# Gated mix of two attentions on one core: the output as f32r products of halves, two octets of a block at a unit's end

## The chip, the cores and the metric

The kernel runs on one core of one Trainium2 chip. The metric is the device time of one execution in microseconds (us). The engines are named as the profile names them: PE (TensorE; its weight loads apart as PEld), DVE (VectorE), ACT (ScalarE), POOL (GpSimd) and SP (SyncE), on which nearly all DMAs are issued. SP issues its DMAs in the order of the program.

## The reference

```python
x = A_x                                            # 1 x 2048 x 512, f32
g = sigmoid((x * gate_w).sum(-1, keepdims=True))
a = attention(x, A_wqkv) @ A_wo                    # 32 heads of 16, full softmax over 2048 keys
b = memory_attention(x, B_wq, B_wk, B_wv) @ B_wo   # 32 heads of 16, four segments of 512 tokens
return g * a + (1 - g) * b
...
# memory_attention, in segment s: causal softmax inside the segment, and a memory of the segments before
o = sig(beta) * (phi(q) @ M) / (phi(q) @ z + 1e-6) + (1 - sig(beta)) * (p @ v)
M = M + phi(k).T @ v; z = z + phi(k).sum()
```

Everything is computed in float32 precision. Where the kernel uses PE's f32r type, an operand is split into a half that f32r holds and a half with the rest, and a product is three matmuls: low by high, high by low, high by high.

## The kernel before

**Stages.** A first stage (to about 320 us) projects x to q, k and v of both sides as three f32r products of halves and writes them to DRAM. The main stage then runs *units*: a unit is one side (A or B), a group g of four heads (0 to 7) and a segment c of 512 query tokens (0 to 3). The units alternate A, B, A, B through the groups of a segment, then the next segment. An A unit has 64 *slots*, a B unit 10; `nS` is the count of all slots. In slot n PE computes one score tile (L645, `st`), of which ACT takes the exponential (L668, `p`), and the score product for a maximum of slot n + 96 (L197, into one of the four `sm` banks), which DVE reduces (L212 for side A, L222 for side B). So every unit's maxima are made 96 slots before its scores. When all maxima of a unit stand, POOL splits them in two halves (L179, L180, `ms`), PE transposes them (L188), ACT copies (L191, `mt`), and SP writes them as further rows into the unit's q (L194, "the rows"); the unit's scores need these rows.

**Bursts.** Every third slot ends a *burst*: there PE computes either values (p times v, L701, up to three or four entries of 128 keys, summed in the bank `ops`) or, if output work is waiting in the list `shared`, four pieces of that; beside it up to one entry of the list `fill` whose slot has come. In the last segment `jam` raises the number of value entries more readily. In `wide`, 60 slots after the last maximum (from slot nS - 94 to nS - 34), a burst is six slots, with up to eight values and three entries of `fill`. Behind the last slot every step is a burst.

**Octets.** When the values of a unit are complete, ACT copies them from `ops`, and SP writes them (L706, `od`). After an odd group the *octet* o = g // 2 (eight heads, 128 rows of attention output) is finished by `octet` in four steps at given slots: SP reads the sums (L744, `rec`) and the values (L751); POOL computes the reciprocal and the factors (L760 to L766) and SP writes them (L767, `rd`); SP reads them spread over the rows (L771, `inv`); POOL multiplies (L774), and on side B adds the memory's part (L776), which after an even B group comes by the same steps as octet "M". The results stay in SBUF, in the tiles `held`.

**Output.** The output of 128 tokens, a *block*, sums over both sides and four octets. `piece` (L784) computes 128 x 128 of it for one octet of one side as four f32 matmuls of 32 tokens side by side in PE's columns; in the profile each such matmul shows as two records. At the end of each A unit of segments 1 to 3 half the columns (two of four pieces wide) of one block of the segment before are computed in `ops`: 16 pieces in four bursts; `leave` (L809) copies them with ACT and SP writes them. In the last segment the ends of six B units also carry output: two quarters of block 3 of segment 2, and octet 0 of the four blocks of the last segment, which `keep` (L817) copies to SBUF.

**Closing.** The rest of the last segment's output, octets 1 to 3, is summed in the four banks of the maxima, which are free by then: 96 pieces from the list `closing`, spread by `close` over `fill` from slot nS - 94 on. The last octet (A, 3) is finished by DVE instead of POOL at the very end; 16 pieces, four additions of the kept part and four writes follow it.

**Queues.** All of this is one program order per engine, written out by the loop at L860; `at(n, f)` (L730) puts f in front of slot n. Loads for a maximum are issued 20 slots ahead of it. Tiles of a tag rotate over its number of buffers, so that a new one waits until the old one's readers are done.

Of the kernel before, what the change touches and what calls it, by code (L numbers as in the profile page):

```python
# [10 lines left out]
F32 = mybir.dt.float32  # L11
# [8 lines left out]
D = 512  # L20
# [26 lines left out]
def gated_mix(ctx, tc, x, xT, wqkv, a_wo, b_wq, b_wk, b_wv, b_wo, beta, gate_w, out):  # L47
# [674 lines left out]
    minus = fr.tile([128, 32], F32, name="minus")  # L722
    nc.gpsimd.memset(minus, -1.0)
    held = {}
    scaled = set()


# [5 lines left out]
    def octet(side, o, c, t0, vector=False):  # L733

        hs = slice(8 * o, 8 * o + 8)
        sums, rows, eng = (dend[c][hs], rdM[c][hs], nc.gpsimd) if side == "M" else (od[side, c][hs, 16], rd[side, c][hs], nc.gpsimd)
        if vector:
            eng = nc.vector
        k = {}

        def load():
            assert side == "M" or {(side, 2 * o, c), (side, 2 * o + 1, c)} <= stored
            k["rec"] = fr.tile([128, 32], F32, tag="rec", name="rec", bufs=3)
            nc.sync.dma_start(k["rec"], sums.rearrange("h (q t) -> h q t", q=16))  # L744
            if side == "M":
                k["v"] = held["M", c, o] = fr.tile([128, CH], F32, tag="vM", name="vM", bufs=2)
            else:
                if (side, c) not in held:
                    held[side, c] = fr.tile([128, NO, CH], F32, tag="v" + side, name="v" + side, bufs=2)
                k["v"] = held[side, c][:, o]  # L750
            nc.sync.dma_start(k["v"], numd[c][:, o] if side == "M" else od[side, c][hs, 0:16].rearrange("h r t -> r h t"))  # L751

        def factors():
            rec = k["rec"]
            if vector:
                eng.reciprocal(rec, rec)
            else:

                r, e = (fr.tile([128, 32], F32, tag=t, name=t, bufs=2) for t in ("rcp", "err"))
                eng.tensor_tensor(r, rec, minus, op=ALU.pow)  # L760
# [6 lines left out]
            nc.sync.dma_start(rows.rearrange("h (q t) -> (h q) t", q=16), k["rec"])  # L767

        def factor():
            k["inv"] = fr.tile([128, CH], F32, tag="inv", name="inv", bufs=3)  # L770
            nc.sync.dma_start(k["inv"], heads(rows))  # L771

        def scale():
            eng.tensor_mul(k["v"], k["v"], k["inv"])  # L774
            if side == "B" and c:
                eng.tensor_add(k["v"], k["v"], held.pop(("M", c, o)))  # L776
            scaled.add((side, o, c))
        for n, f in ((0, load), (10, factors), (17, factor), (28, scale)):
            if t0 is None:
                f()  # L780
            else:
                at(t0 + n, f)

    def piece(ps, side, o, c, b, j, start, stop):  # L784

        assert (side, o, c) in scaled
        for t in range(4):
            nc.tensor.matmul(ps[32 * t:32 * t + 32, 128 * (j % (ps.shape[1] // 128)):128 * (j % (ps.shape[1] // 128)) + 128],  # L788
                             held[side, c][:, o, 128 * b + 32 * t:128 * b + 32 * t + 32], wos[side][:, o, 128 * j:128 * j + 128],
                             start=start, stop=stop, tile_position=(0, 32 * t))  # L790

    def out_rows(c, b):
        return out[c * CH + b * 128:c * CH + (b + 1) * 128, :]
# [1 line left out]
    fill = []  # L795
    shared = []

    def output(c, b, octets, cols, then, bank=ops):

        ps = bank[:, 0:128 * len(cols)]  # L800
        ks = [(side, o, j) for o in octets for side in "AB" for j in cols]
        for i, (side, o, j) in enumerate(ks):
            def f(i=i, side=side, o=o, j=j):
                piece(ps, side, o, c, b, j, i == 0, i == len(ks) - 1)
                if i == len(ks) - 1:
                    then(ps, c, b, cols)
            yield f

    def leave(ps, c, b, cols):  # L809
        w, j0 = 128 * len(cols), 128 * cols[0]  # L810
        t = fr.tile([128, D], F32, tag="res", name="res", bufs=2)
        nc.scalar.copy(t[:, 0:w], ps)
        nc.sync.dma_start(out_rows(c, b)[:, j0:j0 + w], t[:, 0:w])

    part = {}

    def keep(ps, c, b, cols):  # L817
        part[b] = fr.tile([128, D], F32, tag=f"part{b}", name="part")
        nc.scalar.copy(part[b], ps)

    last = NCH - 1
    between = {("A", g, c): (c - 1, g // 2, range(NO), range(2 * (g % 2), 2 * (g % 2) + 2), leave)
               for c in range(1, NCH) for g in range(NG)}
    del between["A", NG - 1, last]
    fill.extend((wide.start, f) for f in output(*between.pop(("A", NG - 2, last)), banks[0]))
    for j in (2, 3):
        between["B", j - 2, last] = (last - 1, 3, range(NO), (j,), leave)
    for b in range(4):  # L830
        between["B", b + 2, last] = (last, b, (0,), range(4), keep)

    for u in units[1:]:
        at(max(0, first[u] - 30), lambda u=u: load_v(u))
    at(100, lambda: load_wo("A", a_wo))
    at(180, lambda: load_wo("B", b_wo))


    closing = [(side, o) for o in range(1, NO) for side in "BA"]
    assert nS - 30 > nS - LEAD + 4  # L840
    def close(n, side, o, b, j):
        def f():
            piece(banks[b], side, o, last, b, j, (side, o) == closing[0] and j == 0, (side, o) == closing[-1] and j == 3)
        fill.append((n, f))
    early = [(k, 0) for k in closing[:4]]
    for (side, o), b in early + [(k, b) for k in closing[:-1] for b in range(4) if (k, b) not in early]:
        for j in range(4):
            close(max(wide.start if ((side, o), b) in early else nS - 30, end[side, 2 * o + 1, last] + 56), side, o, b, j)
# [11 lines left out]
    while n < nS or queue or beside or filled[0] < len(fill):  # L860
        for f in beside.pop(n, []):
            f()
        if n < nS:
            score_part(n)
        m = n + LEAD
        if m < nS:
            loads(m + PRE)

            max_part(m, lambda: banks[m % 4])
        run_todo(m)  # L870
        if n >= nS or n % (2 * BURST if n in wide else BURST) == (2 * BURST if n in wide else BURST) - 1:
            if shared:
                for _ in range(8 if n in wide else 4):
                    shared and shared.pop(0)()
# [18 lines left out]
    assert len(stored) == len(units)  # L893
    for b in range(4):
        for j in range(4):
            close(0, "A", NO - 1, b, j)
            fill.pop()[1]()
        t = fr.tile([128, D], F32, tag="vM" if b % 2 else "res", name="res", bufs=2)
        nc.vector.tensor_add(t, banks[b], part[b])
        (nc.scalar if b % 2 else nc.sync).dma_start(out_rows(last, b), t)  # L900


# [33 lines left out]
```

## Time and profile before

| | us |
|---|---|
| Time, median of 3 runs (lowest to highest) | 1841.38 (1839.18 to 1842.61) |
| Time of the profiled execution | 1840.35 |
| Span of its profile | 1838.6 |
| Mean granted clock of PE | 0.999 |

The busy time of PE, DVE, ACT and POOL in stretches of the main stage, of that execution:

| stretch, us | what runs | PE | DVE | ACT | POOL |
|---|---|---|---|---|---|
| 680 to 1440 (760.0) | segments 1 and 2 | 759.91 | 754.70 | 659.40 | 252.00 |
| 1440 to 1760.5 (320.5) | the last segment, while maxima are made | 320.50 | 312.82 | 272.18 | 111.78 |
| 1760.5 to 1796 (35.5) | no maxima any more; mostly `wide` | 33.30 | 0.00 | 32.92 | 17.50 |
| 1796 to 1817.5 (21.5) | the last scores and values | 21.40 | 0.00 | 17.27 | 4.89 |
| 1817.5 to 1838.6 (21.1) | the rest of the closing and the last octet | 17.16 | 4.00 | 0.59 | 0.00 |

How to read the lines of the profile: "L645" is line 645 of the kernel; "out<-in" are the tiles written and read; "x16" is a count; then come busy time, the mean duration of one in ns, and the idle time of the engine in front of it with what ended it. A line of a timeline begins with the start and the duration in us. SPq rows are the issues of DMAs. Ends of matmuls are modelled, those of DVE, ACT and POOL are not.

### The profile page before, as it was taken

What the parts mean: (1) busy time and instruction counts of PE and PEld (TensorE: products, weight loads), DVE (VectorE), ACT (ScalarE), POOL (GpSimd) and SP (SyncE); (2) the same over time, 40 slices, a digit from 0 to 9 for tenths busy, and PEclk for the clock granted to TensorE, in tenths of its full rate; (3) what the DMA queues carried; (4) which work ended last, traced back from release to release, by engine and by line L of the source; (5) the groups of instructions that cost most, each with busy time, mean ns of one, the idle gap of its engine ahead of it and who ended that gap; (6) DMA issues with size and microseconds to landing.
All of it is one profiled execution on the core that took longest, in us unless ns stands there. A gap on an engine that the chain in (4) does not pass through costs nothing.

```text
span 1838.6 us, 47838 instructions
## 1 busy us (share of the span) xinstructions
PE 1825.7 (99%) x18673; PEld 1001.6 (54%) x18673; DVE 1594.0 (87%) x3331; ACT 1447.4 (79%) x2772; POOL 518.1 (28%) x619
## 2 busy tenths in 40 slices
PE   9999999999999999999999999999999999999999
PEld 7888666545545545454444454444444455555545
DVE  4234677999999999999999999999999999999920
ACT  5445444788888888888888888888888888888894
POOL 3001222104040404242424242424232423242331
PEclk9999999999999999999999999999999999999999
DMA  7568645435343434344444343444344433342421
GB/s 234 195 224 263 210 175 171 137 112 136 89 109 93 113 86 116 103 108 111 111 103 117 103 116 104 116 104 116 104 105 115 116 106 91 107 114 85 114 66 49
DMA packets 124177, 227.40 MB, mean 124 GB/s; under 512 B 34952, under 2 KB 49960, under 8 KB 123440
## 3 DMA queue, kind: packets, MB, share of 16 engines
q1 hardware_dynamic: 122448, 222.68, 42.2%
q8 instruction: 148, 2.42, 0.6%
q0 software_dynamic: 1216, 1.14, 0.2%
q14 instruction: 77, 0.63, 0.1%
q10 hardware_dynamic: 288, 0.52, 0.1%
HBM read 155.52 MB, written 67.52 MB: 121 GB/s over the span
## 4 chain that ended last, share of the span: by engine, by line
PE 96%; ACT 2%; DVE 1%; POOL 1%; issue 0%; DMA 0%; SPq 0%; POOLq 0%; DVEq 0%; ACTq 0%
PE ops L701 32%; PE st L645 28%; PE sm L197 14%; PE pr L295 13%; PE ops L788 6%; PE sm L788 1%; POOL mn L355 1%; PE num L477 1%; ACT p L668 1%; PE mt_ps L188 0%; DMA raw<-wqkv 0%; PE mps L508 0%; ACT ex L362 0%; DVE jk L442 0%; ACT full L350 0%
## 5 line engine op out<-in xcount | busy, mean ns | idle before, releaser
L668 ACT ACTIVATE p<-st 128x512 f32<-128x512 f32 x2276 | 1198.2, 601 | 192.2 <-PE sm L197 149.1
L212 DVE TENSOR_REDUCE pm<-sm 128x1 f32<-128x512 f32 x2048 | 1266.6, 682 | 16.9 <-PE sm L197 16.4
L197 PE MATMUL sm<-kA,qA 48*128 48x512 f32 x2048 | 731.0, 445 | 0.0
L645 PE MATMUL st<-qA,kA 50*128 50x512 f32 x2029 | 668.0, 432 | 1.4 <-ACT mt L191 1.1
L701 PE MATMUL ops<-p,vA 128*17 128x384 f32 (+3 forms) x6872 | 555.3, 424 | 0.0
L645 PEld LDWEIGHTS st<-qA,kA 50*128 50x128 f32 x2029 | 330.7, 185 | 385.3 <-ACT p L668 320.8
L197 PEld LDWEIGHTS sm<-kA,qA 48*128 48x128 f32 x2048 | 332.9, 184 | 21.9 <-issue 7.1
L760 POOL TENSOR_TENSOR rcp<-rec,minus 128x32 f32<-128x32 f32 x43 | 234.1, 5445 | 181.9 <-DMA rec<-dend 137.5
L222 DVE CUSTOM_DVE_ANT_0 rest<-sm,mask 128x128 f32<-128x128 f32 (+3 forms) x512 | 247.9, 484 | 7.6 <-PE sm L197 0.8
L701 PEld LDWEIGHTS ops<-p,vA 128*17 128x17 f32 x6872 | 139.8, 96 | 194.8 <-issue 164.3
L649 POOL TENSOR_SCALAR_AFFINE_SELECT p<-p 128x512 f32<-128x512 f32 x128 | 79.5, 639 | 436.9 <-ACT p L668 433.0
L197 PE MATMUL sm<-kB,qB 48*128 48x128 f32 (+3 forms) x512 | 148.2, 349 | 0.0
L358 DVE TENSOR_TENSOR q<-full,q 128x512 fp32r<-128x512 f32 x64 | 44.4, 694 | 89.9 <-ACT q L351 89.9
L645 PE MATMUL st<-qB,kB 50*128 50x512 f32 (+1 forms) x495 | 109.8, 334 | 0.9 <-ACT p L668 0.9
L645 PEld LDWEIGHTS st<-qB,kB 50*128 50x128 f32 x495 | 70.1, 185 | 58.4 <-ACT p L668 51.4
L197 PEld LDWEIGHTS sm<-kB,qB 48*128 48x128 f32 x512 | 87.5, 186 | 6.4 <-DVE pm L212 2.7
L701 PE MATMUL ops<-p,vB 128*17 128x128 f32 (+3 forms) x1080 | 86.7, 425 | 0.1
L350 ACT COPY full<-pr 128x512 f32<-128x512 f32 x64 | 37.4, 584 | 53.2 <-PE pr L295 52.9
L355 POOL TENSOR_SCALAR mn<-full 128x512 f32<-128x512 f32 x24 | 36.3, 1512 | 101.7 <-ACT full L350 81.3
L788 PE MATMUL ops<-woA,vA 128*32 128x128 f32 x1600 | 64.3, 278 | 0.0
L179 POOL CAST ms<-pm 128x16 fp32r<-128x16 f32 x32 | 6.3, 198 | 204.5 <-DVE pm L222 204.5
L788 PE MATMUL ops<-woB,vB 128*32 128x128 f32 x1600 | 62.1, 273 | 0.0
(157 smaller groups left out, 1489.7 us busy)
## 6 DMA issues: line engine op xcount, KB each, us to landing
kA<-kdA SPq DMA_DIRECT2D x256, 128.0 KB
vA<-vdA SPq DMA_DIRECT2D x31, 544.0 KB
kA<-kdA SPq DMA_DIRECT2D x256, 64.0 KB
qdA<-q SPq DMA_DIRECT2D x32, 256.0 KB
kdA<-q SPq DMA_DIRECT2D x32, 256.0 KB
qdB<-q SPq DMA_DIRECT2D x32, 256.0 KB
qA<-qdA SPq DMA_DIRECT2D x64, 128.0 KB
kdB<-q SPq DMA_DIRECT2D x32, 256.0 KB
```

The costliest lines, as they stand in the source:

```text
L197: nc.tensor.matmul(ps[:, n0:n0 + n], rows(qt[u][:, :, s * 128:(s + 1) * 128], h, 48), rows(k[:, :, k0:k0 + n], h, 48), start=True, stop=True)
L212: nc.vector.tensor_reduce(pm[:, h, s, kc:kc + 1], ps, axis=AX.X, op=ALU.max)
L222: nc.vector.tensor_tensor_reduce(out=tri["rest"][:, 0:w], in0=ps[:, n0:n0 + w], in1=tri["mask"][:, CH - w:], scale=-1.0, scalar=3.0e38, op ...
L295: nc.tensor.matmul(ps, l(a, k), r(b, k), start=(n == 0), stop=(n == 11))
L355: nc.gpsimd.tensor_scalar_min(ph["mn"], full, 0.0)
L358: nc.vector.tensor_sub(q2, full, q1.bitcast(F32))
L645: nc.tensor.matmul(ps[:, n0:n0 + CH - q0], rows(k[:, :, b * 128:(b + 1) * 128], h, 50), rows(q[:, :, q0:], h, 50), start=True, stop=True)
L649: nc.gpsimd.affine_select(out=x, in_=x, pattern=[[0, 4], [1, 128]], base=0, channel_multiplier=-1, compare_op=ALU.is_ge, fill=0.0)
L668: nc.scalar.activation(p[:, h], ps, AF.Exp, scale=SCALE)
L701: nc.tensor.matmul(ops[32 * h:32 * h + 17, q0:q0 + 128 * w], v[:, 17 * h:17 * h + 17], p[:, h, c0:c0 + 128 * w], start=(i == 0), stop=done ...
L760: eng.tensor_tensor(r, rec, minus, op=ALU.pow)
L788: nc.tensor.matmul(ps[32 * t:32 * t + 32, 128 * (j % (ps.shape[1] // 128)):128 * (j % (ps.shape[1] // 128)) + 128], held[side, c][:, o, 12 ...
```

## The change

- `piece` goes. `products` computes the output over all 512 columns at once: for one octet of one side, three f32r matmuls of 128 x 128 weights (the octet's halves) and 512 columns (the halves of the output weights). A block takes 24 of them.
- `octet` ends with a cast and a subtraction that split its result into halves (tile `hl`), and SP writes them to DRAM (`hd`). `held` no longer keeps results in SBUF. The last octet's halves of both sides stay in SBUF.
- At the end of an A unit two octets of a block, not half the columns, are summed: 12 products in three bursts. SP loads their halves 20 slots before the unit's last slot (`load_block`). After an even group `keep` copies the sum to SBUF; after an odd one `leave` copies it, POOL adds the kept sum, and SP writes 128 x 512.
- The last segment's B units carry no output, and `jam` has no case of its own for it. Octet 0 of the last segment joins the closing (120 products with block 3 of segment 2 after the last maximum); the halves of octets 0 to 2 come back from DRAM to buffers of k and q (`load_closed`). `fill` gives four entries a burst in `wide` and behind the last slot, otherwise two.
- The output weights are loaded in eight parts and split by POOL during the first segment.
- At the very end two ACT copies and two DVE copies stand in place of the four additions.

```diff
+    hd = {(s, c): dr.tile([NO, 128, 4, 2, 128], F32, name=f"hd{s}{c}") for s in "AB" for c in range(NCH)}
...
-    def load_wo(side, w):
-        wos[side] = wo.tile([128, NO, D], F32, name=f"wo{side}")
-        nc.sync.dma_start(wos[side], w.rearrange("(o p) d -> p o d", p=128))
+    def load_wo(side, w, o, n):
+        k = {}
+        def load():
+            if o == 0:
+                wos[side] = wo.tile([128, NO, 2, D], F32R, name=f"wo{side}")
+            k["t"] = fr.tile([128, D], F32, tag="v", name="woraw", bufs=2)
+            nc.sync.dma_start(k["t"], w[128 * o:128 * o + 128])
+        def split():
+            h = wos[side][:, o]
+            nc.gpsimd.tensor_copy(h[:, 0], k["t"])
+            nc.gpsimd.tensor_sub(h[:, 1], k["t"], h[:, 0].bitcast(F32))
+        at(n, load)
+        at(n + 8, split)
...
         def scale():
             eng.tensor_mul(k["v"], k["v"], k["inv"])
             if side == "B" and c:
                 eng.tensor_add(k["v"], k["v"], held.pop(("M", c, o)))
+            if side == "M":
+                return
+            t = fr.tile([128, 4, 2, 128], F32R, tag="hl", name="hl", bufs=2)
+            for bs in (slice(0, 2), slice(2, 4)) if vector else (slice(0, 4),):
+                v = k["v"].rearrange("p (b t) -> p b t", b=4)[:, bs]
+                eng.tensor_copy(t[:, bs, 0], v)
+                eng.tensor_sub(t[:, bs, 1], v, t[:, bs, 0].bitcast(F32))
+            if o == NO - 1 and c == NCH - 1:
+                closed[side, o] = t
+            else:
+                nc.sync.dma_start(hd[side, c][o], raw(t))
             scaled.add((side, o, c))
...
-    def piece(ps, side, o, c, b, j, start, stop):
...
+    def products(ps, t, b, side, o, start, stop):
+        for i, (x, w) in enumerate(((1, 0), (0, 1), (0, 0))):
+            yield lambda i=i, x=x, w=w: nc.tensor.matmul(ps, t[:, b, x], wos[side][:, o, w], start=start and i == 0,
+                                                         stop=stop and i == 2)
...
+    def load_block(c, b, os):
+        assert all((side, o, c) in scaled for side in "AB" for o in os)
+        t = fr.tile([128, 2, 2, 2, 128], F32R, tag="blk", name="blk", bufs=2)
+        for i, side in enumerate("AB"):
+            nc.sync.dma_start(raw(t)[:, i, 0:len(os)].rearrange("p o h t -> p o (h t)"),
+                              hd[side, c][os[0]:os[-1] + 1, :, b].rearrange("o p h t -> p o (h t)"))
...
+    def keep(ps, c, b):
+        part[b] = fr.tile([128, D], F32, tag="part", name="part")
+        nc.scalar.copy(part[b], ps)
+
+    def leave(ps, c, b):
         t = fr.tile([128, D], F32, tag="res", name="res", bufs=2)
+        nc.scalar.copy(t, ps)
+        if b in part:
+            nc.gpsimd.tensor_add(t, t, part.pop(b))
+        nc.sync.dma_start(out_rows(c, b), t)
...
+    pairs = range(0, 2), range(2, 4)
+    between = {("A", g, c): (c - 1, g // 2, pairs[g % 2:g % 2 + 1], (keep, leave)[g % 2]) for c in range(1, NCH) for g in range(NG)}
+    for g in (6, 7):
+        del between["A", g, last]
+        at(wide.start - 24, lambda g=g: load_block(last - 1, 3, pairs[g % 2]))
+    fill.extend((wide.start, f) for f in output(last - 1, 3, pairs, leave, banks[0]))
+    for u, (c, b, (os,), _) in between.items():
+        at(end[u] - 20, lambda a=(c, b, os): load_block(*a))
...
+    closing = [(side, o) for o in range(NO) for side in "BA"]
+    def load_closed(side, o):
+        assert (side, o, last) in scaled
+        if o:
+            t = kbuf["A"][knext["A"] % NKA]
+            knext["A"] += 1
+        else:
+            t = qp.tile([128, 2, CH], F32R, tag="q", name="qclosed")
+        t = closed[side, o] = t.rearrange("p a (b h t) -> p (a b) h t", b=2, h=2)
+        nc.sync.dma_start(raw(t), hd[side, last][o])
+    for i, (side, o) in enumerate(closing[:6]):
+        at(nS - 82 + 2 * i, lambda side=side, o=o: load_closed(side, o))
...
-        if n >= first["A", 0, last]:
-            return (len(queue) > 6) + (len(queue) > 13)
...
-                for _ in range(3 if n in wide else 1):
+                for _ in range(4 if n in wide or n >= nS else 2):
...
-        t = fr.tile([128, D], F32, tag="vM" if b % 2 else "res", name="res", bufs=2)
-        nc.vector.tensor_add(t, banks[b], part[b])
+        t = fr.tile([128, D], F32, tag="v" if b % 2 else "res", name="res", bufs=2)
+        (nc.vector.tensor_copy if b % 2 else nc.scalar.copy)(t, banks[b])
         (nc.scalar if b % 2 else nc.sync).dma_start(out_rows(last, b), t)
```

More of the change, by code (lines that the diff above doesn't have):

```diff
@@ L724, in gated_mix @@
     held = {}
+    closed = {}
     scaled = set()
@@ L745, in load @@
             if side == "M":
-                k["v"] = held["M", c, o] = fr.tile([128, CH], F32, tag="vM", name="vM", bufs=2)
+                k["v"] = held["M", c, o] = fr.tile([128, CH], F32, tag="vM", name="vM")
             else:
-                if (side, c) not in held:
-                    held[side, c] = fr.tile([128, NO, CH], F32, tag="v" + side, name="v" + side, bufs=2)
-                k["v"] = held[side, c][:, o]
+                k["v"] = fr.tile([128, CH], F32, tag="v", name="v", bufs=2)
             nc.sync.dma_start(k["v"], numd[c][:, o] if side == "M" else od[side, c][hs, 0:16].rearrange("h r t -> r h t"))
@@ L769, in factor @@
         def factor():
-            k["inv"] = fr.tile([128, CH], F32, tag="inv", name="inv", bufs=3)
+            k["inv"] = fr.tile([128, CH], F32, tag="inv", name="inv", bufs=2)
             nc.sync.dma_start(k["inv"], heads(rows))
@@ L796, in gated_mix @@
     shared = []
[L798 to L810, printed above, removed]
-        t = fr.tile([128, D], F32, tag="res", name="res", bufs=2)
-        nc.scalar.copy(t[:, 0:w], ps)
-        nc.sync.dma_start(out_rows(c, b)[:, j0:j0 + w], t[:, 0:w])
@@ L815, in gated_mix @@
[L815 to L819, printed above, removed]
-    last = NCH - 1
[L824 to L829, printed above, removed]
@@ L830, in gated_mix @@
-    for b in range(4):
-        between["B", b + 2, last] = (last, b, (0,), range(4), keep)
+    blocks = []
+    def load_block(c, b, os):
[4 more added lines that the diff above has]
+                              hd[side, c][os[0]:os[-1] + 1, :, b].rearrange("o p h t -> p o (h t)"))
+        blocks.append(t)
+        loaded_blocks[c, b, os] = len(blocks)
@@ new lines, in gated_mix, with output, f @@
+    loaded_blocks = {}
+    def output(c, b, pairs, then, ps=ops):
+        ks = [(os, o, i) for os in pairs for o in os for i in range(2)]
+        for k in ks:
+            def f(n, k=k):
+                os, o, i = k
+                assert loaded_blocks[c, b, os] > len(blocks) - 2
+                t = blocks[loaded_blocks[c, b, os] - 1][:, i, o % 2].unsqueeze(1)
+                list(products(ps, t, 0, "AB"[i], o, k == ks[0], k == ks[-1]))[n]()
+                if k == ks[-1] and n == 2:
+                    then(ps, c, b)
+            for n in range(3):
+                yield lambda n=n, f=f: f(n)
@@ L839, in gated_mix @@
[L839 to L845, printed above, removed]
+    for i, (side, w) in enumerate((("A", a_wo), ("B", b_wo))):
+        for o in range(NO):
+            load_wo(side, w, o, 30 + 12 * (4 * i + o))
+    closing = [(side, o) for o in range(NO) for side in "BA"]
@@ L846, in gated_mix, with close, f @@
+    def close(n, side, o, b):
+        for i in range(3):
+            def f(i=i):
+                assert (side, o, last) in scaled
+                list(products(banks[b], closed[side, o], b, side, o, (side, o) == closing[0], (side, o) == closing[-1]))[i]()
+            fill.append((n, f))
+    early = [(k, 0) for k in closing[:6]]
     for (side, o), b in early + [(k, b) for k in closing[:-1] for b in range(4) if (k, b) not in early]:
-        for j in range(4):
-            close(max(wide.start if ((side, o), b) in early else nS - 30, end[side, 2 * o + 1, last] + 56), side, o, b, j)
+        close(nS - 66 if ((side, o), b) in early else max(nS - 30, end[side, 2 * o + 1, last] + 60), side, o, b)
@@ L872, in gated_mix @@
             if shared:
-                for _ in range(8 if n in wide else 4):
-                    shared and shared.pop(0)()
+                for _ in range(4):
+                    shared.pop(0)()
             else:
```

15 lines of the change are left out of this document (5 added, 10 removed).

## The prediction, made before the changed kernel ran

> **What bounds the kernel now.** I read the page first, then the busy time by stretches, then the timelines of PE, VectorE (DVE), GpSimd (POOL) and the SP queue around one end of a unit.
>
> ```profile
> PE 1825.7 (99%) x18673; PEld 1001.6 (54%) x18673; DVE 1594.0 (87%) x3331; ACT 1447.4 (79%) x2772; POOL 518.1 (28%) x619
> L212 DVE TENSOR_REDUCE pm<-sm 128x1 f32<-128x512 f32 x2048 | 1266.6, 682 | 16.9 <-PE sm L197 16.4
> ```
>
> PE's 99% says little, since the ends of matmuls are modelled. By stretches (length, then busy time of PE, weight loads, DVE, ACT, POOL) it is plainer:
>
> ```profile
> 680.00:1440.00 760.00, 759.91 (x8577) 372.79 (x8575) 754.70 (x1595) 659.40 (x1279) 252.00 (x291) 1.00 0.41 107
> 1440.00:1760.50 320.50, 320.50 (x4014) 163.34 (x4013) 312.82 (x667) 272.18 (x531) 111.78 (x127) 1.00 0.39 106
> 1760.50:1796.00 35.50, 33.30 (x428) 16.34 (x423) 0.00 (x0) 32.92 (x68) 17.50 (x17) 1.00 0.18 53
> 1796.00:1817.50 21.50, 21.40 (x241) 9.48 (x240) 0.00 (x0) 17.27 (x34) 4.89 (x7) 1.00 0.07 14
> 1817.50:1838.60 21.10, 17.16 (x606) 16.53 (x595) 4.00 (x7) 0.59 (x1) 0.00 (x0) 0.97 0.28 92
> ```
>
> From 680 to 1440 DVE idles 5.3 of 760 us, 0.7%: its maxima set the pace, and work taken from PE there is worth nothing. From 1440, the last segment, it idles 7.7 of 320.5 us, so there PE is part of the bound. After the last maximum (1760.5) PE and ACT share the bound, then PE alone, and the last 21 us are a chain of DMAs.
>
> **The change, part by part.** The profiled execution took 1840.35 us (span 1838.6); the median is 1841.38, and I add that 1.0 at the end.
>
> *One product against one piece.* A product is an f32r matmul of 128 rows, 128 columns of weights and 512 columns; the projections run the same shape, one behind the other (the 18 rows from the first shown to the last are one kind):
>
> ```profile
> 20.03 0.39 PE L295 MATMUL pr<-xh,wkl 128*128 128x512 f32 x1
> ...
> 23.89 0.39 PE L295 MATMUL pr<-xh,wkh 128*128 128x512 f32 x1
> ```
>
> ```profile
> L788 PE MATMUL ops<-woA,vA 128*32 128x128 f32 x1600 | 64.3, 278 | 0.0
> 1830.02 0.69 DVE L774 TENSOR_TENSOR vA<-vA,inv 128x512 f32<-128x512 f32 x1 [6.25 <-DMA inv<-rdA]
> 1830.77 3.92 PE L788 MATMUL sm<-woA,vA 128*32 128x128 f32 x128
> 1834.92 0.69 DVE L899 TENSOR_TENSOR res<-sm,part 128x512 f32<-128x512 f32 x1 [0.29 <-PE sm L788]
> ```
>
> Seventeen intervals in 3.86 us: 0.227 us a product. The last 16 pieces (128 records, eight a piece) took 3.92 us, less 0.28 for the last one's run-out: 0.228 a piece. So the two cost the same, and a block of 128 rows falls from 32 pieces to 24 products, 7.3 to 5.4 us.
>
> *Segments 1 and 2.* A unit's end gives one of four bursts back (four pieces, 0.91 us). DVE sets the pace there: 0. The wider evictions (512 columns for 256) lie on ACT, 659 of 760 us busy: 0.
>
> *Last segment.* B units' ends give no output any more, and A units' three bursts instead of four; the runs are then those of the other segments. If DVE comes to idle 0.7% here as well, 2.2 us, the segment gains 7.7 - 2.2 = **5.4 us**. It cannot gain more, and is worth 0 if something else holds PE.
>
> *After the last maximum.* Octet 0's products now also fall here. By the order of both programs, until the last values stand 24 pieces in eight bursts of the wide stretch and 12 behind, and in the new one 32 and 26. That is 8 x 0.227 = 1.8 us in the wide stretch, where PE is busy 33.3 and ACT 32.9 of 35.5 us, and 26 x 0.227 - 12 x 0.228 = 3.2 us behind it. One burst of each:
>
> ```profile
> 1789.14 1.91 PE L701 MATMUL ops<-p,vA 128*17 128x512 f32 x16
> 1792.53 1.91 PE L701 MATMUL ops<-p,vA 128*17 128x512 f32 x16
> 1800.35 0.40 PE L788 MATMUL sm<-woB,vB 128*32 128x128 f32 x8
> 1802.28 0.40 PE L788 MATMUL sm<-woB,vB 128*32 128x128 f32 x8
> ```
>
> A wide burst takes 3.39 us for six exponentials, a late one 1.93 for three; ACT is busy 17.3 of 21.5 us in the late ones and hides nothing. Bounds 3.2 and 5.0 us; I take **4.1**, half of the wide part hidden behind ACT.
>
> *The end.* After the last values the new program has 50 products in hand, 11.4 us, less than the 12.5 us from 1817.5 until the last factors are multiplied in (1830.02); the chain of DMAs stays the bound. Then come a cast and a subtraction of half a tile on DVE before the first product; by the 0.69 of a whole tile and some start-up, 0.8 us for the two; the second half lies behind products. Twelve products take 2.7 us against 3.9 of the pieces: 0.8 - 1.2 = **-0.4 us** (0 to -0.7).
>
> *The octets' halves, and whom they hold up.* This decides. At the end of an odd A unit POOL, SP and PE work like this (run of the unit ended at 1157.8; SP, then POOL, PE, DVE):
>
> ```profile
> 1157.82 0.34 SPq L706 DMA_DIRECT2D odA<-oraw  x1
> 1165.42 0.36 SPq L813 DMA_DIRECT2D out<-res  x1
> 1168.93 0.34 SPq L767 DMA_DIRECT2D rdA<-rec  x1
> 1171.80 1.02 SPq L771 DMA_DIRECT2D inv<-rdA  x1
> 1183.92 0.34 SPq L767 DMA_DIRECT2D rdB<-rec  x1
> 1187.55 0.53 SPq L771 DMA_DIRECT2D inv<-rdB  x1
> 1193.14 1.43 SPq L194 DMA_DIRECT2D qB<-mt  x2
> ```
>
> ```profile
> 1162.16 5.44 POOL L760 TENSOR_TENSOR rcp<-rec,minus 128x32 f32<-128x32 f32 x1
> 1175.43 1.28 POOL L774 TENSOR_TENSOR vA<-vA,inv 128x512 f32<-128x512 f32 x1 [6.53 <-DMA inv<-rdA]
> 1176.67 5.43 POOL L760 TENSOR_TENSOR rcp<-rec,minus 128x32 f32<-128x32 f32 x1
> 1190.98 1.29 POOL L774 TENSOR_TENSOR vB<-vB,inv 128x512 f32<-128x512 f32 x1 [2.29 <-DMA inv<-rdB]
> 1192.35 1.28 POOL L776 TENSOR_TENSOR vB<-vB,vM 128x512 f32<-128x512 f32 x1
> ```
>
> ```profile
> 1200.07 0.73 PE L197 MATMUL sm<-kA,qA 48*128 48x512 f32 x2
> 1200.41 0.64 PE L645 MATMUL st<-qB,kB 50*128 50x512 f32 x2
> ```
>
> ```profile
> 1201.24 3.08 DVE L212 TENSOR_REDUCE pm<-sm 128x1 f32<-128x512 f32 x5
> ```
>
> The maxima's rows (mt) are issued at 1193.14 and first read by PE's scores at 1200.41. The new program puts on SP, ahead of them, the write of the B octet's halves, which waits until POOL has multiplied, added, cast and subtracted. SP issues in order, so the rows wait too, and behind them the next keys; for the rows PE's scores wait, and behind these, in order, the maxima that feed DVE. How late? POOL's new operations: a 128x512 addition or subtraction 1.28; the cast has no row of its size. Bounds:
>
> ```profile
> L649 POOL TENSOR_SCALAR_AFFINE_SELECT p<-p 128x512 f32<-128x512 f32 x128 | 79.5, 639 | 436.9 <-ACT p L668 433.0
> L355 POOL TENSOR_SCALAR mn<-full 128x512 f32<-128x512 f32 x24 | 36.3, 1512 | 101.7 <-ACT full L350 81.3
> 818.29 0.34 SPq L767 DMA_DIRECT2D rdB<-rec  x1
> 819.73 0.53 SPq L771 DMA_DIRECT2D inv<-rdB  x1
> ```
>
> 0.64 to 1.51 us; I take 1.0, between the two operations of one input. The page GPSIMD Engine Reference of the Trainium skill (Engine selection) calls one-input operations roughly line-rate; L649's row bears that out, L355's, dearer than a two-input 1.28, does not; by the rule the cast would be near 0.64 and the sum below smaller by 0.7 a run.
>
> From a written row of factors to its reading back stand 1.44 us (818.29 to 819.73) to 3.63 (1183.92 to 1187.55); I take 2.0. Now the chain. The output leaves three slots sooner (3 x 0.616 by DVE's row, 1.85) with 0.2 more copying: 1165.42 - 1.85 + 0.2 = 1163.8. POOL adds the kept part, 1.28, ahead of A's reciprocal: 1165.1 instead of 1162.16. To the write of A's factors 6.77: 1171.9; reading begins 1173.9; the product 3.63 later, 1177.5; product, cast, subtraction 3.6: 1181.1. B's reciprocal to its factors 7.25: 1188.3; read 1190.3; product at 3.43 more, 1193.8; product, sum, cast, subtraction 5.05 with gaps: 1198.8. The write 0.4, then the rows' two issues from 1199.2; the second begins near 1199.9 and lands 1.44 later at the soonest: 1201.4 to 1202. PE wanted it at 1200.41: 1.0 to 1.6 us late. DVE is not empty at once: it has the 1200.07 products, until about 1201.85, and needs 0.6 after PE goes on, so the loss is the lateness less 0.9: 0.1 to 0.7 us. With both bounds taken low the lateness is -0.5 and the loss 0; with both high it is 5.6 and the loss 4.7. The late side reaches further: I take 0.8. The order of the new program has this write ahead of the rows in ten runs (four in segment 1, four in 2, two in 3): **+8 us**, 0 to 47. If the cover goes entirely, each further us of lateness costs 10.
>
> *Hidden edits.* The weights' 16 splits on POOL come in the first segment, 12 slots apart, where POOL is idle most of the time; block loads are issued 20 slots ahead with the DMA engines busy 0.41; A's write waits on a POOL result that is 3.6 us old when SP has issued the 16 loads in front: 0, as long as these covers hold.
>
> Sum: 1840.35 - 5.4 + 4.1 - 0.4 + 8 = 1846.7, and with the 1.0 to the median **1848 us**.
>
> **Rivals.**
> (a) *The write is in time.* Cast and readings back at their short ends: no loss. 1841.4 - 5.4 + 4.1 - 0.4 = 1839.7: no change. For it: the loss starts only 0.9 us behind the need. Against it: two bounds must both be short.
> (b) *Faster: PE's relief in the last segment.* As (a), and ACT covers the whole wide part, and the late bursts in part: from 1440 DVE idles 0.7%, 5.4 us, and the tail costs 1.2 or less. It decides from a tail cost below 2: 1837 down to 1835. For it: PE and ACT are within 0.4 us of each other in the wide stretch. Against: the late 3.2 us have no cover.
> (c) *A slow landing.* The rows land behind the 512 KB write in the same queue. In this trace a 16 KB read behind loads came late:
>
> ```profile
> 805.94 0.61 SPq L744 DMA_DIRECT2D rec<-odB  x1
> 811.04 5.43 POOL L760 TENSOR_TENSOR rcp<-rec,minus 128x32 f32<-128x32 f32 x1 [4.44 <-DMA rec<-odB]
> ```
>
> 5.1 us from issue to use. Behind the write I price it 1.2 us above the forecast's, so 10 x 2.0 = 20: 1860. The page DMA: Bandwidth & Descriptors of the Trainium skill (Queues, rings and completion order) has each engine's ring consumed in order, which is this rival; the row above fits it. Against: the rows are 16 KB in all, and the write may be half drained.
> That the products don't run as f32r can't be seen from before; both operands are written as f32r, and I give it nothing of its own.
>
> **Chances.** The forecast 0.38, (c) 0.14, (a) 0.28, (b) 0.20. About 0.2%, 3.7 us, is what a measurement of this kernel tells from no change; the forecast and (c) lie beyond it: slower 0.52, same 0.28, faster 0.20. Range: from (b)'s 1835 to somewhat above (c), where the unknown landing and cast reach, 1867; the forecast's own is 1844 to 1856.
>
> **What would show it.** Right: POOL's cast of 128x512 near 1.0; the rows' issue moved from 7.3 us ahead of the first B scores to about 1; in ten places PE's weight load of B scores waits for a DMA, and DVE idles some 8 us more from 680 on; DVE 99% busy in the last segment outside these places; late bursts of 2.2 us in place of 1.93; 1831.4 as the counterpart of the first product after 1830.02. Wrong: no wait of these scores for a DMA, or idle time of DVE behind POOL's maxima (ms) or block loads instead.

## The result, and the profile after

| | median us | runs | profiled execution: time, span |
|---|---|---|---|
| before | 1841.56 | 4 (1839.18 to 1842.61) | 1840.35, 1838.6 |
| changed | 1862.09 | 4 (1856.16 to 1869.18) | 1869.18, 1867.4 |

The ratio is 1.0115 (95% interval 1.0067 to 1.0163): slower by some 20 us, where 7 were forecast. The changed kernel's four runs lie 13 us apart, the two slower ones at the lower granted clock of PE: 1856.16 and 1856.48 at 0.994 and 0.995, 1867.70 at 0.989, 1869.18 at 0.986. The profile below is that of the last one, 7 us above the median.

The busy time by stretches, cut at the last maximum (columns: window, length, then PE, weight loads, DVE, ACT, POOL, then granted clock, DMA share, GB/s):

```profile
680.00:1440.00 760.00, 750.52 (x6986) 358.59 (x6984) 734.98 (x1552) 645.25 (x1246) 286.89 (x325) 0.98 0.46 126
1440.00:1777.90 337.90, 333.93 (x3150) 159.53 (x3148) 329.74 (x714) 289.57 (x560) 131.08 (x147) 0.99 0.47 129
1777.90:1867.40 89.50, 79.00 (x518) 37.89 (x518) 3.98 (x10) 52.46 (x104) 29.02 (x32) 0.94 0.29 97
```

From 680 to 1440 DVE issues 1552 instructions for 1595: its maxima, which set the pace before, now wait. The last maximum ends at 1777.9 for 1760.5, 17.4 us later, and the stretch behind it takes 89.5 us for 78.1, 11.4 more. Together that is the 28.8 us between the spans.

Who waits (engine, line, what it waited for: us in all, times, longest):

```profile
PE st L661 <- DMA qB<-mt: 11.9, 7, 2.5
PE mt_ps L191 <- POOL ms L183: 6.5, 2, 5.3
DVE pm L215 <- PE sm L200: 36.0, 31, 2.4
```

The first line is the forecast's wait: B scores for the maxima's rows. It was not in the profile of before at all. The second was only named as a sign of being wrong: PE's transposition of the maxima waits for POOL. DVE's waits for PE rose from 16.4 us by 19.6.

The odd run that the forecast walked through, now begun at 1163.86. SP:

```profile
1163.86 0.34 SPq L722 DMA_DIRECT2D odA<-oraw  x1
1178.14 0.34 SPq L782 DMA_DIRECT2D rdA<-rec  x1
1180.67 0.55 SPq L786 DMA_DIRECT2D inv<-rdA  x1
1194.68 0.34 SPq L782 DMA_DIRECT2D rdB<-rec  x1
1196.74 0.53 SPq L786 DMA_DIRECT2D inv<-rdB  x1
1205.26 0.34 SPq L802 DMA_DIRECT2D hdB<-hl  x1
1205.69 1.43 SPq L197 DMA_DIRECT2D qB<-mt  x2
```

Its POOL:

```profile
1170.13 1.27 POOL L859 TENSOR_TENSOR res<-res,part 128x512 f32<-128x512 f32 x1 [1.91 <-ACT res L857]
1171.36 5.45 POOL L775 TENSOR_TENSOR rcp<-rec,minus 128x32 f32<-128x32 f32 x1
...
1200.52 1.29 POOL L789 TENSOR_TENSOR v<-v,inv 128x512 f32<-128x512 f32 x1 [4.98 <-DMA inv<-rdB]
...
1203.25 0.61 POOL L797 CAST hl<-v 128x512 fp32r<-128x512 f32 x1
1203.94 1.29 POOL L798 TENSOR_TENSOR hl<-v,hl 128x512 fp32r<-128x512 f32 x1
```

And its PE:

```profile
1208.17 0.76 PE L661 MATMUL st<-qB,kB 50*128 50x512 f32 x1 [1.59 <-DMA qB<-mt]
```

The rows are issued 0.43 us behind the write of the halves, 2.5 us ahead of the scores that stand still for 1.59 us. What the forecast did not have comes right behind (windows around that wait):

```profile
1190.00:1206.00 16.00, 16.00 (x179) 7.79 (x175) 15.82 (x35) 13.79 (x28) 9.43 (x14) 1.00 0.71 183
1206.00:1209.50 3.50, 1.91 (x14) 0.97 (x14) 2.40 (x7) 1.64 (x5) 0.00 (x0) 0.80 0.41 159
1209.50:1219.00 9.50, 9.50 (x54) 5.42 (x46) 5.47 (x13) 4.99 (x11) 1.87 (x3) 0.50 0.37 110
1219.00:1228.60 9.60, 9.60 (x33) 4.83 (x33) 5.11 (x11) 4.61 (x9) 0.64 (x1) 0.50 0.01 2
1228.60:1240.00 11.40, 11.40 (x115) 4.92 (x111) 11.09 (x24) 10.09 (x20) 4.76 (x1) 1.00 0.51 115
```

For 19 us after the wait PE is granted half its clock. It works through them without a gap, and DVE falls from 99% to 55%. From 1206 to 1228.6, 22.6 us, DVE is busy 13.0: a wait of 1.6 us, with the half clock behind it, cost this run some 9 us of maxima.

The other wait, near the end (POOL, then PE):

```profile
1781.01 1.26 POOL L791 TENSOR_TENSOR v<-v,vM 128x512 f32<-128x512 f32 x1
1782.34 0.61 POOL L797 CAST hl<-v 128x512 fp32r<-128x512 f32 x1
1783.03 1.26 POOL L798 TENSOR_TENSOR hl<-v,hl 128x512 fp32r<-128x512 f32 x1
1784.24 0.20 POOL L182 CAST ms<-pm 128x16 fp32r<-128x16 f32 x1
```

```profile
1785.23 0.64 PE L191 MATMUL mt_ps<-identf,ms 128*32 128x128 f32 x2 [5.30 <-POOL ms L183]
```

The last units' maxima (ms) stand in POOL's order behind octet 2 of side B, whose scale now comes late and is longer by cast and subtraction. DVE finished these maxima at 1777.9; PE gets them at 1785 and works at half clock until 1791.

### The profile page after: what moved, and what is told of

Same layout as the page of the kernel before. It is cut to its first block, busy times and chain, and to the rows that moved or that the text cites. A ratio compares the mean times of both kernels' runs of the same rounds, so it can differ in the third digit from the quotient of the medians.

```text
span 1867.4 us, 41638 instructions
## 1 busy us (share of the span) xinstructions
PE 1836.6 (98%) x15473; PEld 978.9 (52%) x15473; DVE 1590.2 (85%) x3333; ACT 1450.8 (78%) x2768; POOL 604.9 (32%) x708
## 4 chain that ended last, share of the span: by engine, by line
PE 89%; DMA 4%; POOL 2%; ACT 2%; DVE 1%; issue 1%; SPq 0%; DVEq 0%; POOLq 0%; ACTq 0%
PE ops L717 31%; PE st L661 27%; PE sm L200 13%; PE pr L298 10%; PE ops L813 4%; PE sm L813 1%; DMA qB<-mt 1%; ACT p L684 1%; POOL mn L358 1%; DMA raw<-xT 1%; POOL rcp L775 1%; PE num L480 1%; DMA vs<-wqkv 0%; PE mt_ps L191 0%; DMA qdB<-q 0%
## 5 line engine op out<-in xcount | busy, mean ns | idle before, releaser
L200 PE MATMUL sm<-kA,qA 48*128 48x512 f32 x2048 | 742.4, 449 | 0.0
L717 PE MATMUL ops<-p,vA 128*17 128x256 f32 (+3 forms) x7440 | 567.3, 408 | 0.0
L200 PEld LDWEIGHTS sm<-kA,qA 48*128 48x128 f32 x2048 | 337.0, 186 | 23.9 <-issue 7.1
L717 PEld LDWEIGHTS ops<-p,vA 128*17 128x17 f32 x7440 | 154.0, 96 | 205.2 <-issue 163.4
L661 PE MATMUL st<-qB,kB 50*128 50x512 f32 (+1 forms) x495 | 116.8, 350 | 14.3 <-DMA qB<-mt 11.9
L717 PE MATMUL ops<-p,vB 128*17 128x512 f32 (+3 forms) x1024 | 88.9, 443 | 0.1
L789 POOL TENSOR_TENSOR v<-v,inv 128x512 f32<-128x512 f32 x31 | 39.9, 1286 | 125.7 <-DMA inv<-rdB 61.5
```

The lines of the kernel that those rows point to most:

```text
L200: nc.tensor.matmul(ps[:, n0:n0 + n], rows(qt[u][:, :, s * 128:(s + 1) * 128], h, 48), rows(k[:, :, k0:k0 + n], h, 48), start=True, stop=True)
L661: nc.tensor.matmul(ps[:, n0:n0 + CH - q0], rows(k[:, :, b * 128:(b + 1) * 128], h, 50), rows(q[:, :, q0:], h, 50), start=True, stop=True)
L717: nc.tensor.matmul(ops[32 * h:32 * h + 17, q0:q0 + 128 * w], v[:, 17 * h:17 * h + 17], p[:, h, c0:c0 + 128 * w], start=(i == 0), stop=done ...
```

## The experiments

Each kernel was timed against the kernel before on the same chip; differences below are of medians to that one's (1838.94, 1839.82 or 1839.38 us).

**The write put behind the rows.**

```diff
-                nc.sync.dma_start(hd[side, c][o], raw(t))
+                k["t"] = t
...
+        def write():
+            if "t" in k: nc.sync.dma_start(hd[side, c][o], raw(k["t"]))
...
-        for n, f in ((0, load), (10, factors), (17, factor), (28, scale)):
+        for n, f in ((0, load), (10, factors), (17, factor), (28, scale), (28 + 8, write)):
```

> Every octet's halves are written eight slots after their scale, in a step of its own, so on SP the write stands behind the maxima's rows that it stood ahead of. Order theory (rows held in SP's order by the write, which waits for POOL): rows are issued 5 to 7 us ahead of the B scores in all runs of the loop, PE's waits for them (21.4 us in the changed kernel's profile) go to under 4 us, DVE is back at 99% in 1100:1300, the half-clock stretches are gone, and the time is 1844 (1840 to 1849). Ring theory (the 512 KB write slows whatever lands near it, wherever it stands): waits for rows or block loads stay above 12 us and the time is over 1855. Load theory (the loss is in the POOL adds, block loads and products themselves): 1855 to 1862.

Measured: 1843.37 us (1837.74 to 1848.34, 10 runs), ratio 1.0021 (1.0011 to 1.0032), +4.4. PE's waits and the middle stretch:

```profile
PE mt_ps L191 <- POOL ms L183: 5.3, 1, 5.3
PE st L661 <- DMA qB<-mt: 2.0, 3, 0.8
```

```profile
680.00:1440.00 760.00, 757.76 (x7184) 365.36 (x7180) 753.57 (x1597) 662.62 (x1280) 289.63 (x331) 1.00 0.46 129
```

DVE is back at 1597 instructions and the clock at 1.00. The bytes, the products, the casts and the block loads are all still there, so none of them is the loss in the middle; the place of the write is. The tail's 5.3 us stays.

**The last scale put behind the maxima.**

```diff
+        for n, f in (..., (28 + 20 * ((side, o, c) == ("B", 2, NCH - 1)), scale)):
```

> Only octet 2 of side B in the last segment is scaled twenty slots later, so that POOL makes the last units' maxima before it and SP issues their rows before its write. Order theory on POOL: PE's wait of 5.3 us for the maxima at 1780 goes, the value burst after it runs at full clock, the rest stays: 1862 - 5 - 1.5 = 1855 (1852 to 1858 at a median over the same spread of the clock). Rival (the last stretch waits for something else anyway, such as the read of the octet or ACT): no change, 1860 to 1864.

Measured: 1855.38 us (1845.07 to 1859.12, 5 runs), +16.4. The long wait for ms is gone (1.8 us are left, in another place, at 640); the rows' 12.3 us in 9 places stay. As expected, though its runs spread over 14 us.

**Both.** The write at 36 slots, for octet 2 of side B in the last segment at 49, its scale at 48.

> The two together: writes eight slots after their scales, and octet 2 of side B in the last segment scaled twenty slots later. Order theory: 1838 (1834 to 1843), that is the changed kernel without its stalls; at or below the kernel before if the last segment's gain of 5.4 us outweighs the tail's 58 products. Load theory: 1850 to 1858.

Measured: 1835.80 us (1832.35 to 1844.98, 10 runs), ratio 0.9984 (0.9972 to 0.9997), -3.1: below the kernel before. By stretches:

```profile
680.00:1440.00 760.00, 757.01 (x7178) 364.83 (x7170) 752.98 (x1596) 661.98 (x1279) 289.46 (x330) 1.00 0.47 129
1440.00:1752.30 312.30, 311.14 (x2955) 148.43 (x2954) 309.07 (x669) 271.82 (x526) 128.27 (x144) 1.00 0.46 130
1752.30:1834.60 82.30, 76.16 (x518) 37.11 (x518) 3.99 (x10) 52.14 (x104) 28.71 (x30) 1.00 0.33 110
```

This kernel, called the third kernel from here on, is the change almost without its waits (3.5 us for rows are left, in four places), and so the check of the forecast's other terms (below). The four kernels fit each other: the place of the write is worth 16.4 + 3.1 = 19.5 us by the second and third, the tail 4.4 + 3.1 = 7.5 by the first and third. The second kernel's ratio lies between 1.0052 and 1.0107, so that the first of these is good to some 5 us.

**The write on POOL's queue.** `nc.gpsimd.dma_start` for `nc.sync.dma_start`, nothing else.

> The write is issued by POOL's own queue at the same place, so it moves the same bytes at the same moment but holds nothing of SP. Order theory: as with the write put later, 1844 (1840 to 1850), if POOL's issue is under 1.5 us; the tail's wait of 5 us for the maxima stays or grows by that issue. Ring theory (bytes near the rows are what costs): 1856 or more, with rows landing over 4 us after their issue.

Measured: 1849.99 us (1846.47 to 1863.12, 5 runs), +11.1. In its profile the rows are gone from PE's larger waits, so order on SP and not the bytes was at work. But PE waits for the maxima (first row), and the issue stands on POOL (second):

```profile
PE mt_ps L191 <- POOL ms L183: 8.7, 2, 6.7
```

```profile
1203.59 0.65 POOL L802 DMA_DIRECT2D hdB<-hl  x1 [0.30 <-POOL hl L798]
```

Each issue takes POOL 0.65 us and 0.30 of waiting before, and lengthens the tail's queue from 5.3 to 6.7. The time was at the upper end of what order theory gave; moving the write to the engine that others wait for is no remedy.

**PE kept busy while the rows are late.** To the kernel with the last scale moved:

```diff
+            for _ in range(6 if c and g % 2 == 0 and (g, c) != (6, NCH - 1) and j == 0 else 0):
+                nc.tensor.matmul(ps[:, 0:128], identf, identf, start=True, stop=True)
```

> As e2_last_scale_late, with six 128x128 products of the identity (0.27 us each by the four at 329.0 of the changed kernel, 1.6 us together) ahead of the first B scores of the eleven units whose rows come late; they go into the score's own bank, which the score then overwrites. PE is as late as before, but not idle. Clock theory (the waits of 1.2 to 2.6 us make the chip halve PE's clock for 3.4 to 20 us, and that costs more than the waits): no half-clock stretch between 680 and 1740, a clock of 0.998 or more, and 1836 + 11 x (1.6 - 0.9) = 1844 (1840 to 1848), that is 10 us faster than e2 in spite of 18 us more of work for PE. Rival (the waits themselves cost all, and the clock falls for another reason): 1855 to 1866, with half-clock stretches as in e2.

Measured: 1850.64 us (1848.57 to 1853.09, 5 runs), +10.8: 5.6 us better than the kernel it was made from, with 18 us more work on PE, yet 7 us above what was expected. The middle stretch of that kernel, then of this one:

```profile
680.00:1440.00 760.00, 750.89 (x7014) 358.41 (x7006) 737.24 (x1556) 647.34 (x1250) 286.58 (x325) 0.98 0.46 126
```

```profile
680.00:1440.00 760.00, 759.57 (x7196) 369.13 (x7195) 746.27 (x1575) 654.45 (x1265) 288.68 (x328) 1.00 0.46 128
```

The clock stays at 1.00 (five runs at 0.997 to 0.999, against 0.990 to 0.997), the spread shrinks from 14 to 4.5 us, and DVE regains half of the instructions that it lost (1556 to 1575, with 1596 in the third kernel). So the half clock behind these waits follows from PE's idleness and is a part of the loss, not the whole. The rest, 10.8 + 3.1 = 13.9 us over eleven runs, is 1.26 a run for a delay of 1.6: by this estimate the maxima that DVE has in hand cover some 0.35 us, not 0.9. The 5.6 us are not all that the half clock cost, since the products delay PE by 18 us in all where its waits for rows had been 12.3.

**Without POOL's addition.**

```diff
         if b in part:
-            nc.gpsimd.tensor_add(t, t, part.pop(b))
+            part.pop(b)
```

> The changed kernel without POOL's addition of the kept half of a block (L859, 1.28 us, once in an odd run); the output then lacks the first two octets of each block of the first three segments. Chain theory (rows are late because POOL's work ahead of the write has grown by this add, the cast and the subtraction, 3.2 us in all and twice the last two): taking 1.3 us and the wait of pow behind it out of the chain brings the rows 1.3 to 3 us forward, PE's waits for them go from 11.9 us to under 4, and the time is 1846 (1842 to 1851), with the tail's wait of 5 us kept. Rival (the chain's start is set by the write and read of the sums, and POOL's add falls into that gap): the time stays at 1855 or more.

Measured: 1838.67 us (1836.33 to 1845.17, 10 runs), ratio 0.9995 (0.9985 to 1.0005), -1.2; 7 us below what was expected. The same run, SP and POOL:

```profile
1164.81 0.34 SPq L722 DMA_DIRECT2D odA<-oraw  x1
...
1202.93 0.34 SPq L802 DMA_DIRECT2D hdB<-hl  x1
1203.37 1.43 SPq L197 DMA_DIRECT2D qB<-mt  x2
```

```profile
1169.13 5.44 POOL L775 TENSOR_TENSOR rcp<-rec,minus 128x32 f32<-128x32 f32 x1
```

The reciprocal starts 4.3 us after the unit's end instead of 7.5, the rows go out at 38.6 instead of 41.8, and PE does not wait for them, although the write still stands 0.44 us ahead of them on SP. An addition of 1.28 us moves the chain by 3.2, because in POOL's order it holds the reciprocal until ACT has evicted the block. That this write is no trouble when it is early also speaks against a slow landing.

**The old rule for values in the last segment.** The third kernel, with the two lines of `jam` that the change took out.

> As e3_both, with the two lines of jam that let the last segment put one or two more values into a burst, as the kernel before did. If the last segment's gain (8.4 us between maximum 1700 and the last, 5.4 forecast) comes from these runs being as the others', the time is 1835.8 + 5 = 1841 (1838 to 1844), and DVE idles 6 us there again. If it comes from the pieces that no longer stand in the B units' slots, the time stays at 1836 (1834 to 1838).

Measured: 1840.88 us (1837.41 to 1843.59, 10 runs), +1.1. From 1440 to its last maximum:

```profile
1440.00:1756.50 316.50, 315.81 (x2893) 147.98 (x2891) 311.92 (x669) 271.59 (x527) 128.96 (x145) 1.00 0.47 130
```

The same 669 instructions take 4.2 us more than in the third kernel: half of the last segment's gain is this rule. The other half is left, by exclusion, to the output that the runs no longer carry; no run tried that alone. The idle DVE time grew less than expected (4.6 us against 3.2).

**The block loads put behind the rows too.** The third kernel, with `end[u] - 14` for `end[u] - 20`.

> As e3_both, with each unit's block loads issued six slots later, behind the maxima's rows on SP where they stood ahead of them. In e3 PE still waits 3.5 us for rows at 1014.7 and 1293.2 and two more places, where two block loads (0.9 us of SP) stand between the key loads and the rows. If SP's issue time is what is left of the lateness: the waits go under 1 us and the time is 1834 (1831 to 1836). Rival (the remaining waits are the rows' landing or POOL's maxima): no change, 1835 to 1837; or the blocks now come late for the products: PE waits for them and the time is over 1838.

Measured: 1833.18 us (1832.31 to 1837.79, 5 runs), ratio 0.9961 (0.9948 to 0.9975), -6.6: the fastest against its own kernel before. PE's waits for rows fall from 3.5 us to 0.7. In its profiled execution, its slowest run, PE waits once for the maxima, 2.2 us at 640, behind an octet of the first segment.

**That octet moved as well.** Side B's octets of the first segment are scaled and written six slots later.

> As e8_blocks_after_rows, with side B's octets of the first segment scaled and written six slots later, which puts one octet's scale behind the maxima of a unit on POOL (the one at 640 in e8, where PE waited 2.2 us for the maxima, 1.25 us at 637.5 in the changed kernel). If that order is a wait in most executions: 1831 (1829 to 1833), 2 us under e8, and no wait for the maxima in the loop. Rival (that wait falls in a few executions only, since the chain before it starts late by chance): as e8, 1832 to 1834.

Measured: 1833.48 us (1831.75 to 1835.33, 6 runs), ratio 0.9967 (0.9955 to 0.9980), -5.9. The wait for the maxima is gone from its profile, and no gain shows in the median: the rival, a wait that few executions have, fits better. Among the kernels with the write put later the wait stands in one profile of four. The six profiles with the write in its first place all have it, 1.0 to 2.0 us at 638 to 641, so a small part of what that place cost lies here.

**The changed kernel again.**

> The changed kernel again, on the chip of e9, so that the two can be compared and its spread is known. If the half-clock stretches after PE's waits are chance in length, as theory has it, the times spread over 10 us and more and fall with the granted clock (0.995 gave 1856, 0.986 to 0.989 gave 1868): median 1862 (1855 to 1868), against a spread of 4 us of the kernel before. Rival (two levels that hold for a chip or a session): all runs at one of the two.

Measured: 1862.33 us (1854.25 to 1863.84, 5 runs), ratio 1.0115 (1.0097 to 1.0132), +23.0. The fastest run had a clock of 0.995, the slowest two 0.989, so the spread belongs to the executions and not to a chip.

## Why the prediction was right, and where it was short

The sign, the place and the mechanism were right: on SP the write of the B octet's halves stands ahead of the maxima's rows, which come late by POOL's longer chain. The size was not: 1848 for 1862. That lies outside the forecast's own 1844 to 1856; the whole range reached 1867 for a slow landing and a dear cast, neither of which came, so that the time fell inside it was luck.

*Lateness.* The chain was followed to within 0.7 us. Counted from the unit's write, forecast and measured: reciprocal of A 7.3 and 7.5, A's factors out 14.1 and 14.3, B's factors 30.5 and 30.8, B's product 36.0 and 36.7, write of the halves 41.0 and 41.4. Lateness was put at 1.0 to 1.6; this run shows 1.59 and the seven waits a mean of 1.7. The cast was 0.61 for the 1.0 taken, and the time saved there was lost again at the readings back. The page GPSIMD Engine Reference of the Trainium skill (Engine selection) calls one-input operations roughly line-rate; the cast agrees with that, at half of the 1.28 of two inputs. Such waits showed in seven places (eight and nine in two other profiles), not in ten.

*The price of being late* is the step that failed: +8 as ten times 0.8, "the loss is the lateness less 0.9". Measured, the place of the write is worth 19.5 us (18.6 by the repeated kernel against the first experiment: 23.0 - 4.4). Two things stood in its place. The cover was some 0.35 us a run and not 0.9, by the kernel with the busy waits (an estimate). And four of the seven waits bring PE's clock down, for 3.4 to 20 us, which the forecast had not considered. By that cover seven waits of 1.7 cost some 9.5 us, which leaves about 10 of the 19.5 to the clock; no run parts the two cleanly. It worked with a constant clock although the stretches it quoted carry that column. At half clock PE, which ran at 99 to 100% before, cannot feed DVE.

*The tail after the last maximum* was put at +4.1 - 0.4 = 3.7. Without waits it is 82.3 - 78.1 = 4.2: right. In the changed kernel it was 11.4, since the scale of octet 2 stood ahead of the last maxima on POOL. The forecast named this wait only among the signs of being wrong. Having found that POOL's chain ends some 5 us later, it asked who waits behind it on SP and not who waits behind it on POOL itself. Two experiments price it at 6.6 to 7.5 us (23.0 - 16.4, and 4.4 + 3.1).

The late bursts were forecast at 2.2 us for 1.93; from the first to the last of these (scores at the head of nine bursts) it is eight in 17.33 us, 2.17:

```profile
1824.92 0.72 PE L661 MATMUL st<-qA,kA 50*128 50x512 f32 x3
...
1842.25 0.73 PE L661 MATMUL st<-qA,kA 50*128 50x512 f32 x3
```

The last chain was not right: from the last factors' product to the end stand 9.0 us (1858.43 to 1867.4) where 8.6 did (1830.02 to 1838.6), +0.4 for -0.4. The cast and the subtraction cost what was forecast (the first product starts 1.54 us after that one, for 0.75), but the twelve products took 3.0 us and not 2.7, and from the last copy to the end stand 3.6 us where 3.0 did:

```profile
1858.43 0.69 DVE L789 TENSOR_TENSOR v<-v,inv 128x512 f32<-128x512 f32 x1 [5.11 <-DMA inv<-rdA]
1859.97 3.02 PE L813 MATMUL sm<-woA,hl 128*128 128x512 f32 x12 [0.69 <-DVE hl L798]
```

*The last segment* was put at -5.4 with "it cannot gain more". Without waits, 669 instructions of DVE take 312.3 us where 667 took 320.5: -8.2. The bound was wrong because busy time is no constant: with the same work DVE was busy 312.82 us before and 309.07 after. A reduction that follows another overlaps it (2048 of 0.682 us were busy 1266.6 us, 0.618 each); one that waited counts in full. So the idle time of a waiting engine is understated: of the 8.2 us, 4.5 came out of the 7.7 that showed as idle and 3.7 out of busy time.

*Hidden edits* at nothing: in the middle the third kernel has 1596 instructions of DVE for 1595 before, so the f32r products, wider evictions, splits and writes cost nothing there, and save nothing. The block loads were not free, since SP issues them just ahead of the rows: moved, they gave 1835.80 - 1833.18 = 2.6 us, or 3.5 against each one's own before.

*The rivals.* (c), rows that land slowly behind the 512 KB write, named nearly the right time for a wrong reason: the write still ahead of the rows but early (no addition on POOL), or on another queue, brings no wait. The rows' landing says it directly: behind the write PE read them 2.5 us after their issue began (1205.69 to 1208.17), in the third kernel, with block and value loads right ahead of them and no write, 4.9 us (1196.62 to 1201.54). (a) and (b) needed the write in time; that is what the third kernel made, and it came out at -3.1, between the two. The sum without the write's term was -1.7.

## What to carry to other kernels

A short operation put into an in-order engine's chain has to be followed to everything behind it, on that engine first: 1.28 us of POOL in the wrong place cost 24 us here (+23.0 against -1.2), and moving issues and scales by a few slots, with the same work, turned +23.0 into -6.6. Where an engine runs at 99%, a wait is not priced by its length alone: ask what covers it, and what the clock does after it. What is only stored for later is issued behind what someone waits for.

## What the runs showed of the hardware

PE's clock fell to half after waits that are short. Three more places of the changed kernel's profile (the waits, then the windows behind them):

```profile
925.61 0.46 PE L661 MATMUL st<-qB,kB 50*128 50x512 f32 x1 [1.84 <-DMA qB<-mt]
1019.93 0.47 PE L661 MATMUL st<-qB,kB 50*128 50x512 f32 x1 [2.45 <-DMA qB<-mt]
1310.75 0.76 PE L661 MATMUL st<-qB,kB 50*128 50x512 f32 x1 [2.00 <-DMA qB<-mt]
```

```profile
925.70:945.00 19.30, 19.30 (x157) 9.64 (x157) 18.26 (x40) 16.71 (x33) 3.65 (x5) 1.00 0.28 88
...
1020.30:1023.80 3.50, 3.50 (x20) 1.13 (x22) 1.86 (x3) 1.80 (x4) 0.00 (x0) 0.51 0.39 116
...
1310.50:1317.30 6.80, 6.55 (x31) 2.45 (x33) 2.77 (x6) 2.87 (x6) 0.65 (x1) 0.50 0.23 61
```

A wait of 1.84 us was followed by no lower clock, one of 2.45 by 3.5 us at half, one of 2.00 by 6.8, one of 1.59 by 19 (the run above). The profile's other three waits for rows were 2.06, followed by 6.8 us at half, and 1.17 and 0.80, followed by none. The kernel with the last scale moved has one of 1.18, followed by 3.3 us at half, the third kernel one of 1.28, followed by none. With matmuls in the place of the waits the clock stayed at 1.00 from 680 to 1440. Waits are not the only occasion: the kernel before has 3.4 us at half too, from 513, and in the 8 us ahead of that PE's longest wait is 0.18 us. The page TensorE: Matmul & The Clock Gate of the Trainium skill (HAM oscillation) warns of gaps over about 3.4 us. These lie below that, so here the measurement decides: a gap of half that length can be enough. What decides it, and how long the low clock lasts, is open.
